# State split that carries the softmax scale, work moved from VectorE to ScalarE and GpSimd, and a new list of steps

## The chip, the cores and the metric

The kernel runs on one core of a Trainium2 chip. The metric is the device time of one execution in microseconds (us). The names of the engines are those of the profile: PE is TensorE's matmul side and PEld its weight load, DVE is VectorE, ACT is ScalarE, POOL is GpSimd, SP is the engine that issues most transfers.

## The reference

Eight batches of eight heads: tokens x (512 x 64 a head) read from a small state (32 x 64 a head), the state reads from the tokens, and the 4608 rows that come out (8 x 512 of the tokens, 8 x 32 of the states, the heads side by side in 512 columns) go through two feed-forward blocks.

```python
def attn(x, state):                      # x [8, 8, 512, 64], state [8, 8, 32, 64]
    scale = 1.0 / np.sqrt(64)
    scores = scale * np.matmul(x, state.transpose(0, 1, 3, 2))
    scores = scores - scores.max(-1, keepdims=True)
    a = np.exp(scores)
    a /= a.sum(-1, keepdims=True) + 1e-09
    xread = np.matmul(a, state)
    scores2 = scale * np.matmul(state, x.transpose(0, 1, 3, 2))
    a2 = softmax(scores2)                # written out as above
    sread = np.matmul(a2, x)
    return np.concatenate([xread, sread], axis=2)

def moe(x, w_in, w_out, g_ln):           # x [4608, 512], w_in [512, 1024], w_out [1024, 512]
    h = x @ w_in
    e = np.exp(h - h.max(-1))
    solu = h * e / (e.sum(-1) + 1e-09)
    ln = (solu - mean(solu)) / np.sqrt(var(solu) + 1e-06) * g_ln
    return ln @ w_out

def moe2(x, w_in, w_out):                # w_in [512, 2048], w_out [2048, 512]
    h = x @ w_in
    return np.maximum(0.01 * h, h) @ w_out
```

## The kernel before

**Precision and shapes.** Most products are computed from pairs of a high and a low part: `hi` is the value as the narrower type fp32r, `lo` is what is left of it, and `mm3` (line 136) issues three passes, hi by hi, hi by lo and lo by hi. A value is split by a copy into `hi` on ACT and a subtraction into `lo` on DVE or POOL. The scores of batches 0 and 1 (`PLAIN_S`) are plain fp32 products without a low part, and their rows of `st` and `sw` show two passes to a product.

**Stages.** Behind the scaled and transposed tokens (`at_xT`, line 335: `xT_hi`, `xT_lo`) and the state as a block matrix (`at_state`, line 293: `stp` in fp32, `stq` in two parts) come the scores of the state (`at_scores`, line 356: `st`, from them `a2`, transposed by PE as `a2t` in `at_a2T`) and the softmax of the tokens (`at_soft1`, line 392: the maximum `mx`, the subtraction into `ee`, the exponential, the sum `sm`, its reciprocal, the product). `at_sw1` and `at_sw2` form the state times the first weights, `w_in` (`sw`), so that `h1` (line 542) has the first product of the block straight from the softmax `a1T`. `solu_norm` (line 502) turns a strip of 128 rows of `h` into the normalised `e`; its statistics sit in little tensors `sn(b, r)` of one or two columns. `turn`, `carry` (line 620) and `x2` (line 648) transpose the strip, split it into `hi` and `lo` in place in `ln`, and multiply by `w_out`. Weights come in raw and are narrowed and split by `narrow_w_in`, `split_w_in` (line 244), `narrow_w_out` and `split_w_out` (line 281). This first phase ends near 400 us; the second block, on sums and differences of quarters of the tokens, fills the rest of the span.

**What sets the order.** Each of these functions is a generator that stops at every `yield`. The string `PROGRAM` (line 1418) is a list of tokens; a letter names the function, the numbers its arguments, and each occurrence carries the generator to its next `yield`: `T` is `at_xT`, `Z` `at_state`, `S` `at_scores`, `U` `at_soft1`, `A` and `B` `at_a2T` and `at_a1T`, `Y` and `W` `at_sw1` and `at_sw2`, `h` `h1`, `V`, `C` and `X` `turn`, `carry` and `x2`, `i` and `j` narrow and split `w_in`, `o` and `p` narrow and split `w_out`. The loop that reads it is at line 1382. Each engine gets its instructions in the order in which the list issues them (`PINNED`) and works through them strictly in that order; nothing is chosen at run time. Transfers are issued by SP's queue in the list's order too.

**At the start** POOL makes the identity matrix for PE's transpositions, clears the two z buffers of the state, all of `stq` (128 x 2048 columns) and `stp`, and PE's first work is the transposition of the state of batch 0.

Of the kernel before, what the change touches and what calls it, by code (L numbers as in the profile page):

```python
# [16 lines left out]
ALU = mybir.AluOpType  # L17
# [12 lines left out]

PLAIN_S = (0, 1)
CARRIED = (1, 2, 3, 4, 5, 6, 7)
LO_ROW_DVE = ()
# [5 lines left out]
def f32(ap):  # L39
    return ap.bitcast(F32)  # L40
# [26 lines left out]
def attn_solu_leaky_kernel(  # L67
# [88 lines left out]
    make_identity(tc.nc, ident)  # L156
    nhalf = slot("nhalf", [P, 1], F32, "nhalf")
    nc.gpsimd.memset(nhalf, -0.5)
# [8 lines left out]
    nc.gpsimd.memset(f32(stq), 0.0)  # L167
# [76 lines left out]
    def split_w_in(k):  # L244
# [5 lines left out]
        nc.gpsimd.tensor_tensor(t[:, 1], w, f32(t[:, 0]), ALU.subtract)  # L250
# [30 lines left out]
    def split_w_out(k):  # L281
# [4 lines left out]
        nc.gpsimd.tensor_tensor(lo, w, f32(hi), ALU.subtract)  # L286
# [6 lines left out]
    def at_state(b, g):  # L293
        for _ in (0,):
# [5 lines left out]
            for m in range(2):  # L300
# [5 lines left out]
                if b in PLAIN_S:  # L306
                    nc.scalar.copy(stp[:, 2 * g + m, d], pt[:, c])
                else:
                    yield from split(stq[:, 0, 2 * g + m, d], stq[:, 1, 2 * g + m, d], pt[:, c])
# [25 lines left out]
    def at_xT(b, hp):  # L335
        if hp == 0:
            att["xT_hi"] = slot("q2", [P, NHP, S], F32 if b in PLAIN_S else F32R, f"xT_hi{b}")
        if b not in PLAIN_S:
# [4 lines left out]
            nc.scalar.activation(hi, t, AF.Copy, scale=SCALE)  # L343
            yield
            nc.vector.scalar_tensor_tensor(lo, t, SCALE, f32(hi), ALU.mult, ALU.subtract)
# [10 lines left out]
    def at_scores(b, g):  # L356
# [26 lines left out]
        nc.vector.tensor_scalar_mul(a2[:, g, :], a2[:, g, :], r2)  # L383
# [8 lines left out]
    def at_soft1(b, g):  # L392
# [8 lines left out]
        nc.vector.tensor_tensor(e3, v, mx.unsqueeze(2).to_broadcast([P, 16, NS]), ALU.subtract)  # L401
# [5 lines left out]
        nc.vector.tensor_scalar_add(sm, sm, EPS_SM)  # L407
# [94 lines left out]
    def solu_norm(key, hp_):  # L502
# [31 lines left out]
        nc.vector.tensor_scalar_mul(c2, cf, rs)  # L534
# [85 lines left out]
    def carry(b, h):  # L620
# [21 lines left out]
        for u in range(2):  # L642
            yield
            hi, lo = (t[:, 4 * h + 2 * u : 4 * h + 2 * u + 2] for t in ln_t[b])
            w = nc.vector if (b, h, u) in LO_ROW_DVE else nc.gpsimd
            w.tensor_tensor(lo, f32(lo), f32(hi), ALU.subtract)
# [772 lines left out]
    a0 i0 i0 i0 z0. i0 i0 Z0.1 Z0.0 Z0.0 a1 i1 x0.0 T0.0 i1 a3 a2 T0.1 T0.0 g Z0.0 i1 i1 i1 z1.  # L1419
    T0.1 S0.0 i3 i2 Y0.0.0 i3 i3 Z0.1 S0.0 S0.0 S0.0 Y0.0.0 Y0.0.1 Y0.0.1 Z0.1 i3 i2 i3 i2 i2 i2  # L1420
    Z1.1 Z1.1 Z1.1 x0.1 T0.2 Z1.0 Z1.0 T0.3 T0.2 T0.3 S0.1 U0.0 j3 Y0.1.0 S0.1 S0.1 Z1.0 U0.1 b0
    o0 Y1.0.0 z2. Z2.0 S0.0 S0.1 S0.1 b2 Y0.1.0 U0.0 o0 S0.0 U0.0 S0.1 Y1.0.0 Z2.0 Y1.0.1 A0.0
    A0.0 A0.1 A0.1 R0 U0.1 Z2.1 o0 U0.0 U0.1 o0 j3 o2 b1 o1 U0.1 o2 R0 Y1.0.1 R0 U0.0 Y0.1.1
    B0.0 R0 Z2.1 Z2.1 Z2.0 o1 Y1.1.1 U0.1 Y1.1.1 B0.1 o0 o1 o2 o1 j2 h0.1 Y0.1.1 h0.1 x1 o2 Z2.1
# [163 lines left out]
```

## Time and profile before

| | us | share of the span |
|---|---|---|
| median of 3 runs (1131.33, 1136.59, 1137.94) | 1136.59 | |
| profiled execution, device time | 1131.78 | |
| its span | 1130.0 | 100% |
| PE busy | 1095.8 | 97% |
| PEld busy (overlaps PE) | 909.5 | 80% |
| DVE busy | 892.2 | 79% |
| POOL busy | 609.2 | 54% |
| ACT busy | 569.0 | 50% |

The profiled execution is 4.8 us under the median of the three. Busy time counts instructions and is an average over stages that differ: DVE is at 9 and 8 tenths in the first eighth of the span and at 5 to 8 behind it. A row of a timeline says when a group of instructions began and how long it took, a row of the list of lines how long one takes on average, and a row of the waits how long an engine stood still and which result it stood for.

### The profile page before, as it was taken

Reading aid. Unit: us, or ns where it says so; the run is one execution under the profiler, and the core shown is the slowest. Engines: PE = TensorE matmul, PEld = TensorE weight load, DVE = VectorE, ACT = ScalarE, POOL = GpSimd, SP = SyncE. Lnnn points to the kernel's source line nnn. Section 1 sums busy time; section 2 is a strip of 40 time slices with the busy share of each in tenths; the row PEclk is TensorE's granted clock in tenths of the full one; section 3 lists DMA queues with packets and bytes.
Section 4 is the critical chain, followed back from the end, with each engine's and each line's share of the span. In section 5 each row is a group of like instructions: output and inputs, shape, how many; then the busy total and the mean of one; then the engine's idle time right before and its main releaser. Section 6 shows DMA issues by size and latency. Waiting matters only on the chain.

```text
span 1130.0 us, 16127 instructions
## 1 busy us (share of the span) xinstructions
PE 1095.8 (97%) x5872; PEld 909.5 (80%) x5872; DVE 892.2 (79%) x1374; ACT 569.0 (50%) x907; POOL 609.2 (54%) x439
## 2 busy tenths in 40 slices
PE   6999999999999999999999989999999999999997
PEld 2555587888788778888888879998889998899987
DVE  7999988887985585667776977888967778776777
ACT  5687687676677374544234343334443335433331
POOL 2234353262462645576647268878665655745463
PEclk9999999999999999999999999999999999999999
DMA  9447989789589856646449577666794658646352
GB/s 303 126 116 195 212 220 214 202 183 266 162 206 269 241 189 227 219 146 228 159 153 333 219 273 277 244 258 236 280 357 192 261 205 316 231 187 253 131 196 75
DMA packets 170647, 247.48 MB, mean 219 GB/s; under 512 B 93128, under 2 KB 129992, under 8 KB 159560
## 3 DMA queue, kind: packets, MB, share of 16 engines
q1 hardware_dynamic: 170568, 246.45, 67.3%
q8 instruction: 46, 0.75, 0.3%
q14 instruction: 33, 0.27, 0.1%
HBM read 171.97 MB, written 74.45 MB: 218 GB/s over the span
## 4 chain that ended last, share of the span: by engine, by line
PE 57%; DMA 2%; issue 1%; POOL 1%; DVE 1%; ACT 0%; POOLq 0%; DVEq 0%; SPq 0%; ACTq 0%
PE hX L53 15%; PE oX L53 11%; PE o L53 10%; PE hY L53 7%; PE oY L53 5%; PE hZ L53 4%; PE oZ L53 2%; PE h L53 2%; PE x L53 1%; DMA xbT<-xts 1%; DMA wf<-wf2s 1%; DMA xbB<-xs 1%; POOL gb L53 0%; DVE C L53 0%; POOL xbT L53 0%
## 5 line engine op out<-in xcount | busy, mean ns | idle before, releaser
L53 DVE TENSOR_TENSOR oacc<-oacc,oX 128x512 f32<-128x512 f32 x171 | 116.0, 683 | 51.2 <-PE oX L53 50.4
L53 PE MATMUL x<-ln,w_out_hi 128*128 128x512 f32 (+1 forms) x512 | 152.7, 382 | 1.4 <-DVE sw L53 1.4
L53 PE MATMUL hX<-xbT,w 128*128 128x512 f32 x576 | 150.2, 396 | 1.8 <-ACT C L53 1.4
L53 ACT COPY C<-hX 128x512 f32<-128x512 f32 x96 | 56.2, 586 | 145.8 <-PE hX L53 142.6
L53 PEld LDWEIGHTS hX<-xbT,w 128*128 128x128 f32 x576 | 103.1, 188 | 21.9 <-ACT C L53 2.4
L53 PEld LDWEIGHTS x<-ln,w_out_hi 128*128 128x128 f32 x512 | 93.4, 188 | 20.7 <-DVE sw L53 1.6
L53 PE MATMUL h<-sw,a1T 128*128 128x512 f32 x352 | 102.8, 437 | 2.5 <-DVE sw L53 1.3
L53 PE MATMUL x<-ln,w_out_lo 128*128 128x512 f32 (+1 forms) x256 | 97.0, 379 | 0.0
L53 POOL TENSOR_TENSOR gb<-C,gb 128x512 fp32r<-128x512 f32 (+1 forms) x43 | 69.2, 1613 | 44.9 <-ACT gb L53 22.5
L53 POOL TENSOR_TENSOR gc<-C,gc 128x512 fp32r<-128x512 f32 (+1 forms) x43 | 67.7, 1577 | 43.8 <-ACT gc L53 20.1
L53 PEld LDWEIGHTS h<-sw,a1T 128*128 128x128 f32 x352 | 64.7, 188 | 30.5 <-issue 14.3
L53 DVE TENSOR_TENSOR C<-C,hY 128x512 f32<-128x512 f32 x64 | 43.9, 686 | 48.8 <-ACT C L53 42.3
L53 DVE SCALAR_TENSOR_TENSOR C<-C 128x512 f32<-128x512 f32 x88 | 78.7, 896 | 0.4
L53 POOL TENSOR_TENSOR ln<-ln,ln 128x1024 fp32r<-128x1024 f32 x28 | 69.1, 2480 | 17.9 <-ACT ln L53 17.8
L53 DVE TENSOR_TENSOR oacc<-oacc,o 128x512 f32<-128x512 f32 x70 | 46.1, 682 | 25.5 <-PE o L53 25.2
L53 DVE TENSOR_TENSOR oacc<-oacc,oY 128x512 f32<-128x512 f32 x93 | 63.1, 681 | 2.4 <-PE oY L53 1.6
L53 PEld LDWEIGHTS x<-ln,w_out_lo 128*128 128x128 f32 x256 | 48.2, 188 | 9.7
L53 POOL TENSOR_TENSOR gb<-S,gb 128x512 fp32r<-128x512 f32 x27 | 43.1, 1604 | 18.2 <-ACT gb L53 11.0
L53 POOL TENSOR_TENSOR gc<-S,gc 128x512 fp32r<-128x512 f32 x26 | 38.9, 1507 | 25.7 <-ACT gc L53 18.8
L53 PE MATMUL hY<-xbT,w 128*128 128x512 f32 x192 | 49.7, 394 | 0.2 <-DVE C L53 0.2
L53 PE MATMUL hX<-xbB,w 128*128 128x512 f32 x192 | 49.6, 393 | 0.0
L53 PE MATMUL hY<-xbB,w 128*128 128x512 f32 x192 | 49.5, 393 | 0.0
(672 smaller groups left out, 2774.4 us busy)
## 6 DMA issues: line engine op xcount, KB each, us to landing
w<-w2s SPq DMA_DIRECT2D x24, 1792.0 KB, 10.1
shared<-wo2s SPq DMA_DIRECT2D x24, 768.0 KB, 4.4
wi<-wsc SPq DMA_DIRECT2D x14, 1024.0 KB, 6.1
exd<-v SPq DMA_DIRECT2D x14, 1024.0 KB, 6.0
ln<-exd SPq DMA_DIRECT2D x56, 256.0 KB, 6.0
xs<-xo SPq DMA_DIRECT2D x34, 256.0 KB, 4.0
raw<-in_moe_w_in SPq DMA_DIRECT2D x8, 1024.0 KB, 6.2
raw<-in_moe_w_out SPq DMA_DIRECT2D x8, 1024.0 KB, 6.4
```

The source lines that it names most:

```text
L53: done = call(*args, **kw)
```

## The change

Six things change together.

1. **Scale.** For batches 2 to 7 the factor 1/8 leaves `at_xT`: `xT_hi` becomes a plain copy of the transposed tokens and `xT_lo` a plain subtraction. It goes into the two parts of the state (`stq`: a scaled copy on ACT, and one fused scale and subtract on DVE in place of a subtract), and, since the tokens' softmax is then multiplied by a state that is scaled, into the divisor of that softmax (`sm`, one fused add and multiply in place of an add).
2. **Off DVE.** For batches with two-part scores the subtraction into `xT_lo` and the subtraction of the maximum in `at_soft1` go to POOL; for batches 1 to 7 the two-column product `c2` in `solu_norm` goes to POOL; for all batches the division of `a2` goes to ACT.
3. **Pieces.** The POOL subtractions of 1024 columns in `split_w_in`, `split_w_out` and `carry` become two of 512 columns each, every piece a step of its own in the list.
4. **Warm-up.** 24 products of zeros with zeros run on PE before anything else, on 512 columns of `stq` that POOL clears first; the identity and the rest of `stq` follow.
5. **New list.** The steps of the first phase, up to about 400 us, stand in a new order; the list behind it is the old one.
6. Per engine the totals go from 1340 to 1260 instructions on DVE, 823 to 839 on ACT, 439 to 541 on POOL and 5656 to 5680 on PE.

```diff
+WARM = 24
-    make_identity(tc.nc, ident)
-    nc.gpsimd.memset(nhalf, -0.5)
 ...
-    nc.gpsimd.memset(f32(stq), 0.0)
+    nc.gpsimd.memset(f32(stq[:, 0, :2, :]), 0.0)
+    warm = bank("warm")
+    zeros = stq[:, 0, :2, :].rearrange("p a b -> p (a b)")
+    for _ in range(WARM):
+        nc.tensor.matmul(warm, zeros[:, :P], zeros, start=True, stop=True)
+    drop("warm")
+    make_identity(tc.nc, ident)
+    nc.gpsimd.memset(nhalf, -0.5)
+    nc.gpsimd.memset(f32(stq[:, 0, 2:, :]), 0.0)
+    nc.gpsimd.memset(f32(stq[:, 1]), 0.0)
 ...                                             # split_w_in; split_w_out alike
-        nc.gpsimd.tensor_tensor(t[:, 1], w, f32(t[:, 0]), ALU.subtract)
+        for i in range(2):
+            if i:
+                yield
+            c = slice(i * 512, (i + 1) * 512)
+            nc.gpsimd.tensor_tensor(t[:, 1, c], w[:, c], f32(t[:, 0, c]), ALU.subtract)
 ...                                             # at_state, batches 2 to 7
-                    yield from split(stq[:, 0, 2 * g + m, d], stq[:, 1, 2 * g + m, d], pt[:, c])
+                    hi, lo = (stq[:, j, 2 * g + m, d] for j in range(2))
+                    nc.scalar.activation(hi, pt[:, c], AF.Copy, scale=SCALE)
+                    yield
+                    nc.vector.scalar_tensor_tensor(lo, pt[:, c], SCALE, f32(hi), ALU.mult, ALU.subtract)
 ...                                             # at_xT, batches 2 to 7
-            nc.scalar.activation(hi, t, AF.Copy, scale=SCALE)
-            yield
-            nc.vector.scalar_tensor_tensor(lo, t, SCALE, f32(hi), ALU.mult, ALU.subtract)
+            nc.scalar.copy(hi, t)
+            yield
+            nc.gpsimd.tensor_tensor(lo, t, f32(hi), ALU.subtract)
 ...                                             # at_scores
-        nc.vector.tensor_scalar_mul(a2[:, g, :], a2[:, g, :], r2)
+        nc.scalar.activation(a2[:, g, :], a2[:, g, :], AF.Copy, scale=r2)
 ...                                             # at_soft1
-        nc.vector.tensor_tensor(e3, v, mx.unsqueeze(2).to_broadcast([P, 16, NS]), ALU.subtract)
+        w = nc.vector if b in PLAIN_S else nc.gpsimd
+        w.tensor_tensor(e3, v, mx.unsqueeze(2).to_broadcast([P, 16, NS]), ALU.subtract)
 ...
-        nc.vector.tensor_scalar_add(sm, sm, EPS_SM)
+        if b in PLAIN_S:
+            nc.vector.tensor_scalar_add(sm, sm, EPS_SM)
+        else:
+            nc.vector.tensor_scalar(sm, sm, EPS_SM, SCALE, ALU.add, ALU.mult)
 ...                                             # solu_norm
-        nc.vector.tensor_scalar_mul(c2, cf, rs)
+        if key[0] in CARRIED:
+            nc.gpsimd.tensor_tensor(c2, cf, rs.to_broadcast([P, 2]), ALU.mult)
+        else:
+            nc.vector.tensor_scalar_mul(c2, cf, rs)
 ...                                             # carry
-        for u in range(2):
-            yield
-            hi, lo = (t[:, 4 * h + 2 * u : 4 * h + 2 * u + 2] for t in ln_t[b])
-            w = nc.vector if (b, h, u) in LO_ROW_DVE else nc.gpsimd
-            w.tensor_tensor(lo, f32(lo), f32(hi), ALU.subtract)
+        for u in range(4):
+            yield
+            hi, lo = (t[:, 4 * h + u] for t in ln_t[b])
+            nc.gpsimd.tensor_tensor(lo, f32(lo), f32(hi), ALU.subtract)
 ...                                             # PROGRAM, its first line
-    a0 i0 i0 i0 z0. i0 i0 Z0.1 Z0.0 Z0.0 a1 i1 x0.0 T0.0 i1 a3 a2 T0.1 T0.0 g Z0.0 i1 i1 i1 z1.
+    a0 i0 i0 i0 i0 a1 i1 x0.0 z0. T0.0 T0.1 a3 i0 T0.0 a2 Z0.0 i1 Z0.0 Z0.0 Z0.1 Z0.1 i1 T0.1
```

What the new list and the moved operations do to the engines' queues is seen at three places. The first is PE behind the first scores, of the kernel before: `sw_g_n` is the state times half g of the rows and half n of the columns of `w_in` (batch 0, and later batch 1 under the same name), `sw_141` the narrowed first half of `w_in` that such a product reads and `sw_192` the second half; `zt` is the transposed state, `xt` the transposed tokens, `st` the scores of the state, `a2t` the transposed softmax of them.

```order
L53 MATMUL sw_0_0_197<-sw_141,stp 128x512 x2
L53 MATMUL sw_0_1_208<-sw_141,stp 128x512 x2
L53 MATMUL zt_1_219<-ident,z_84 128x128
L53 MATMUL xt_2_227<-ident,xn 128x128 x4
L53 MATMUL zt_0_232<-ident,z_84 128x128
L53 MATMUL xt_3_235<-ident,xn 128x128 x4
L53 MATMUL st_1_242<-xT_hi_164,stp 128x512 x2
L53 MATMUL sw_1_0_250<-sw_192,stp 128x512 x2
L53 MATMUL sw_0_0_265<-sw_141,stp 128x512 x2
L53 MATMUL zt_0_272<-ident,z_83 128x128
L53 MATMUL sw_0_1_288<-sw_141,stp 128x512 x2
L53 MATMUL a2t_0_291<-ident,q_93 128x128 x4
```

The same place of the change; here `sw_168` is the first half of `w_in` and `sw_216` the second.

```order
L53 MATMUL sw_0_0_219<-sw_168,stp 128x512 x2
L53 MATMUL sw_0_1_222<-sw_168,stp 128x512 x2
L53 MATMUL xt_3_230<-ident,xn 128x128 x4
L53 MATMUL xt_2_241<-ident,xn 128x128 x4
L53 MATMUL zt_0_258<-ident,z_79 128x128
L53 MATMUL st_1_272<-xT_hi_185,stp 128x512 x2
L53 MATMUL zt_1_280<-ident,z_79 128x128
L53 MATMUL sw_0_1_290<-sw_168,stp 128x512 x2
L53 MATMUL sw_1_1_310<-sw_216,stp 128x512 x2
L53 MATMUL sw_1_0_322<-sw_216,stp 128x512 x2
L53 MATMUL a2t_1_334<-ident,q_120 128x128 x4
L53 MATMUL a2t_0_339<-ident,q_120 128x128 x4
```

Before, the first product that reads the second half of `w_in` (`sw_1_0_250`) came right behind the second scores; now a product of batch 1 that reads the first half (`sw_0_1_290`) comes between, both products of batch 0 that read the second half stand together, and `a2t` follows them at once. (Ahead of these rows stand the 24 warm-up products, and the tokens are transposed before the state.)

The second place is POOL in the stretch in which the halves of the softmax of batch 1 (`ee`) meet the last pieces of `w_out_lo` and the statistics `sn` of batch 1, of the kernel before:

```order
L53 TENSOR_TENSOR ee_739<-ee_739,sm_0_794 128x512
L53 TENSOR_TENSOR w_out_lo<-w_out_f,w_out_hi 128x1024
L53 TENSOR_TENSOR ee_739<-ee_739,sm_1_822 128x512
L53 TENSOR_TENSOR a1T_840<-q_93,a1T_840 128x512
L53 TENSOR_TENSOR w_out_lo<-w_out_f,w_out_hi 128x1024
L53 TENSOR_TENSOR a1T_840<-q_93,a1T_840 128x512
L53 TENSOR_SCALAR sn(1, 3)_800<-sn(1, 3)_800 128x1
L53 TENSOR_TENSOR sn(1, 3)_800<-sn(1, 3)_800,nhalf 128x1
L53 TENSOR_SCALAR sn(1, 1)_816<-sn(1, 1)_816 128x1
L53 TENSOR_TENSOR sn(1, 1)_816<-sn(1, 1)_816,nhalf 128x1
L53 TENSOR_TENSOR w_out_lo<-w_out_f,w_out_hi 128x1024 x2
```

and of the change, where batch 2's tokens are already being split (`xT_lo`, four subtractions):

```order
L53 TENSOR_TENSOR xT_lo<-q_120,xT_hi_627 128x512 x4
L53 TENSOR_TENSOR w_out_lo<-w_out_f,w_out_hi 128x512
L53 TENSOR_TENSOR ee_772<-q_120,mx_1_773 128x512
L53 TENSOR_TENSOR w_out_lo<-w_out_f,w_out_hi 128x512
L53 TENSOR_SCALAR sn(1, 2)_701<-sn(1, 2)_701 128x1
L53 TENSOR_TENSOR sn(1, 2)_701<-sn(1, 2)_701,nhalf 128x1
L53 TENSOR_TENSOR ee_772<-q_120,mx_0_803 128x512
L53 TENSOR_TENSOR sn(1, 2)_701<-sn(1, 2)_701 128x2
L53 TENSOR_SCALAR sn(1, 0)_649<-sn(1, 0)_649 128x1
L53 TENSOR_TENSOR sn(1, 0)_649<-sn(1, 0)_649,nhalf 128x1
L53 TENSOR_TENSOR ee_772<-ee_772,sm_1_848 128x512
L53 TENSOR_TENSOR sn(1, 0)_649<-sn(1, 0)_649 128x2
```

The pieces of `w_out_lo` are half as large and stand between operations that the scores and the softmax of batch 2 need, and each strip's chain of `sn` ends on POOL with the two-column product that DVE had.

The third place is DVE in the same stretch, before:

```order
L53 TENSOR_TENSOR sw_780<-sv_3_1_918,sw_780 64x512
L53 SCALAR_TENSOR_TENSOR xT_lo<-q_93,xT_hi_930 128x512
L53 STREAM_TRANSPOSE q_93<-xv_499 128x512
L53 TENSOR_TENSOR sw_758<-sv_2_1_938,sw_758 64x512
L53 TENSOR_TENSOR sw_758<-sv_3_1_918,sw_758 64x512
L53 TENSOR_TENSOR sw_780<-sv_2_0_933,sw_780 64x512
L53 SCALAR_TENSOR_TENSOR xT_lo<-q_93,xT_hi_930 128x512
L53 TENSOR_SCALAR sn(1, 3)_800<-sn(1, 3)_800 128x2
L53 TENSOR_TENSOR sw_780<-sv_2_1_938,sw_780 64x512
L53 TENSOR_SCALAR sn(1, 1)_816<-sn(1, 1)_816 128x2
```

and in the change:

```order
L53 STREAM_TRANSPOSE q_120<-xv 128x512
L53 TENSOR_TENSOR sw_784<-sv_3_0_906,sw_784 64x512
L53 COPY srT<-sr_941 64x4x32
L53 TENSOR_TENSOR sw_732<-sv_3_1_913,sw_732 64x512
L53 STREAM_TRANSPOSE v_928<-e(1, 2)_719 128x32x32
L53 TENSOR_TENSOR sw_732<-sv_3_0_906,sw_732 64x512
L53 STREAM_TRANSPOSE v_928<-e(1, 1)_935 128x32x32
L53 TENSOR_TENSOR sw_732<-sv_2_0_980,sw_732 64x512
L53 TENSOR_TENSOR sw_732<-sv_2_1_984,sw_732 64x512
L53 STREAM_TRANSPOSE v_928<-e(1, 3)_875 128x32x32
L53 STREAM_TRANSPOSE q_120<-xv_493 128x512
L53 TENSOR_TENSOR sw_784<-sv_2_1_984,sw_784 64x512
```

The rows `xT_lo` and the two-column `sn` rows are gone from DVE's queue, and the transpositions `q` of the tokens and the sums `sw` stand directly behind one another.

## Rows read from the trace of the kernel before

**Rows 1.** Windows: from:to, length, busy us (count) of five engines, PEclk, DMA, GB/s.
```profile
0.00:25.00 25.00, 14.68 (x40) 6.91 (x41) 17.59 (x21) 12.21 (x23) 6.13 (x12) 1.00 0.97 299
25.00:125.00 100.00, 94.24 (x371) 54.81 (x369) 97.41 (x185) 75.47 (x135) 33.29 (x31) 1.00 0.61 156
125.00:350.00 225.00, 219.78 (x1007) 174.72 (x1008) 194.62 (x371) 162.92 (x267) 91.58 (x83) 1.00 0.85 211
350.00:1130.00 780.00, 767.09 (x4458) 673.08 (x4456) 582.58 (x799) 318.42 (x484) 478.23 (x314) 1.00 0.63 227
```

**Rows 2.** Waits of PE, 25 to 425 us: us in total, times, longest.
```profile
PE st L53 <- DVE xT_lo L53: 1.7, 2, 1.1
PE tr L53 <- DVE stq L53: 1.5, 1, 1.5
PE sv L53 <- DVE sw L53: 1.5, 1, 1.5
...
PE h L53 <- DVE sw L53: 1.3, 2, 0.8
```

**Rows 3.** Timelines of DVE, POOL, PE, 117 to 126: start, length, [idle <- releaser].
```profile
117.64 0.68 DVE L53 SCALAR_TENSOR_TENSOR xT_lo<-q,xT_hi 128x512 fp32r<-128x512 f32 x1
118.24 2.34 DVE L53 TENSOR_SCALAR sn(1, 3)_800<-sn(1, 3)_800 128x2 f32<-128x2 f32 x1
...
121.11 0.21 DVE L53 TENSOR_SCALAR sn(1, 1)_816<-sn(1, 1)_816 128x2 f32<-128x2 f32 x1
...
117.65 2.91 POOL L53 TENSOR_TENSOR w_out_lo<-w_out_f,w_out_hi 128x1024 fp32r<-128x1024 f32 x1
...
122.79 0.40 PE L53 MATMUL st<-xT_lo,stq 128*128 128x512 f32 x1
123.03 1.03 PE L53 MATMUL st<-xT_hi,stq 128*128 128x512 f32 x2
125.21 0.51 PE L53 MATMUL st<-xT_lo,stq 128*128 128x512 f32 x1 [1.15 <-DVE xT_lo L53]
```

**Rows 4.** Lines by form, DVE, 0 to 425: busy us, mean ns | idle before.
```profile
L53 DVE SCALAR_TENSOR_TENSOR xT_lo<-q,xT_hi 128x512 fp32r<-128x512 f32 x24 | 16.7, 699 | 0.8 <-ACT xT_hi L53 0.8
...
L53 DVE TENSOR_TENSOR ee<-q,mx 128x512 f32<-128x512 f32 x16 | 10.8, 679 | 0.0
...
L53 DVE TENSOR_SCALAR q<-q,sa 128x512 f32<-128x512 f32 x16 | 7.9, 500 | 0.2
...
L53 DVE TENSOR_TENSOR stq<-zt,stq 128x64 fp32r<-128x64 f32 x24 | 4.5, 209 | 0.2
...
L53 DVE TENSOR_SCALAR sn(6, 1)_2749<-sn(6, 1)_2749 128x2 f32<-128x2 f32 x1 | 2.4, 2357 | 0.2 <-POOL sn(6, 1)_2749 L53 0.2
```

**Rows 5.** Lines by form, POOL and then ACT, 0 to 425 us.
```profile
L53 POOL TENSOR_TENSOR ln<-ln,ln 128x1024 fp32r<-128x1024 f32 x28 | 69.1, 2480 | 17.9 <-ACT ln L53 17.8
L53 POOL TENSOR_TENSOR ee<-ee,sm 128x512 f32<-128x512 f32 x16 | 18.0, 1126 | 42.9 <-DVE sm L53 23.0 <-DVE sn(3, 1)_1450 L53 8.7 <-ACT junk L53 5.6
L53 POOL TENSOR_TENSOR a1T<-q,a1T 128x512 fp32r<-128x512 f32 x12 | 15.7, 1319 | 13.7 <-ACT a1T L53 13.7
...
L53 POOL TENSOR_TENSOR sn(0, 1)_401<-sn(0, 1)_401,nhalf 128x1 f32<-128x1 f32 x1 | 0.6, 556 | 0.1
...
L53 ACT ACTIVATE w_out_f<-w_out_f,gln 128x512 f32<-128x512 f32 x8 | 5.3, 715 | 0.0
```

**Rows 6.** Timelines of the start: PE, then DVE, then POOL.
```profile
12.29 2.95 PE L53 MATMUL st<-xT_hi,stp 128*128 128x512 f32 x4
...
21.28 1.98 PE L53 MATMUL st<-xT_hi,stp 128*128 128x512 f32 x4 [0.36 <-ACT xT_hi L53]
23.57 3.67 PE L53 MATMUL sw<-sw,stp 128*128 128x512 f32 x8 [0.30 <-DVE sw L53]
...
22.20 1.23 DVE L53 SCALAR_TENSOR_TENSOR sw<-raw_in,wi 128x1024 uint32<-128x1024 uint32 x1
...
1.73 1.80 POOL L53 MEMSET stq<- 128x2048 f32 x1
```

## What the change should do to the time

> **What bounds the kernel now.** I read the busy time of each engine by stretches first [rows 1]. Before 350 us TensorE (PE) is idle for 10.3 us (0 to 25), 5.8 us (25 to 125) and 5.2 us (125 to 350), 21.3 us in all, under 2% of the span. That is about the ceiling of this change: behind 350 us the list of steps is nearly the old one, and PE is busy there for 767.1 of 780 us.
>
> The same rows name the engine that paces PE early on: VectorE (DVE) is busy 97.4 of 100 us in 25 to 125 and 194.6 of 225 us after that, against 75.5 and 162.9 us for ScalarE (ACT) and only 33.3 and 91.6 us for GpSimd (POOL). The waits of PE after 25 us agree: four of the rows that stand highest there end on a DVE result and hold 6.0 us in six waits [rows 2]; what each of them waits for either leaves DVE in this change or stands in its queue behind something that leaves.
>
> Then I looked at what DVE did just before such a wait [rows 3]. At 118.24 a two-element multiplication on DVE lasts 2.34 us; one of the same kind at 121.11 takes 0.21 us. It began while a 128x1024 GpSimd subtraction ran (117.65, 2.91 us) and ended with it. Everything behind it on the DVE queue moved back, among it the xT_lo for which PE then stood still until 125.21 (1.15 us). An ordinary DVE operation on two SBUF tensors started at 117.64 under the same subtraction and kept its 0.68 us. So a small DVE scaling can be held for the length of a GpSimd piece, and a plain two-input operation is not. The list by form has another held one, 2.36 us [rows 4].
>
> A wait costs PE a little more than its own length: passes that follow each other start 0.24 us apart and last 0.40 us (122.79, 123.03), so 0.16 us of overlap is lost, and the first pass after the wait lasts 0.51 us (125.21). That is 0.27 us on top of each wait.
>
> **The change, part by part.** Off DVE go 24 xT_lo subtractions (0.699 us each, 16.8), 16 scalings of a2 (0.500, 8.0), 12 of the 16 subtractions of the maximum (0.679, 8.1) [rows 4] and 28 two-element scalings at 0.21 us (5.9) [rows 3], with at least the 4.3 us by which two of them were held. Sum 43 us: DVE falls in 25 to 350 from 292.0 to 249 of 325 us, from 90% to 77%. The 24 scaled splits of the state have no row. The subtraction that each replaces takes 0.209 us; an operation of the new kind on eight times the columns takes 0.699 us [rows 4]. Size and input are the old ones, so I take 0.21 us, no change; the upper end, 24 x 0.49 = 12 us, would still leave DVE at 80%.
>
> Onto ACT go 16 scalings; the nearest row is a scaling by a vector, 0.715 us [rows 5], 11.4 us. ACT rises from 238.4 to 250 of 325 us, 77%: as full as DVE then, not as DVE was.
>
> Onto POOL go 24 xT_lo subtractions at 1.319 us (the a1T row has their shape and types), 31.7; 12 subtractions of a broadcast maximum at 1.126 us (the ee row has their shape, also with a broadcast operand), 13.5; and 28 two-element products, between the 0.21 us of DVE and the 0.556 us of the costliest kind of small GpSimd operation in the rows; I take 0.3, 8.4, with 15.6 as the upper end. 36 subtractions of 1024 columns at 2.480 us become 72 at 1.319, 36 x 0.158 = 5.7 us more [rows 5]. Sum 59 us: POOL rises in 25 to 350 from 124.9 to about 184 us, 57%. What the split buys is that a held DVE operation waits for 1.3 us at most instead of 2.5.
>
> Folding the scale into the state's split and into the divisor costs nothing more: it sits in a ScalarE copy and in a small DVE operation that are there already, and that have other work of PE in front of them. The copy into xT_hi stays on ACT at its size.
>
> At the start 24 warm-up passes run while PE would wait for data. GpSimd clears two z tiles and 512 columns of stq first (a quarter of the 1.80 us row), so they begin near 1.9 us. At 0.24 us a pass they end at 7.7 us, at half that rate at 13.4; the nearest row is one at half rate, so I take a mixture, 10 us, about when x arrives. What they are for shows in two rows [rows 6]: the same four score passes take 2.95 us at 12.29 and 1.98 us at 21.28. A pass of that size takes 0.46 us (3.67 us for eight), so 2.95 is two passes at the lower of the two levels (1.2 GHz) and two at 2.4 GHz, though the clock column of the stretch says 1.00 [rows 1]. Gain at most 1.0 us. The Trainium skill (TensorE: Matmul & The Clock Gate, Part 1) has the clock follow how busy the array has been lately and fall back after idling. By that rule a pause between the warm-up and the arrival of x could give the 1.0 us back; no row here shows such a fall.
>
> The new list also moves one sw product of batch 1 (four passes, 1.8 us) ahead of the first sw that needs the second half of w_in. That half leaves DVE at 23.4 us, and PE stood 0.30 us for it [rows 6]. The DVE work in front of it is the same in both lists, so PE wins what it gets done before 23.5 us. The transposition of a2, soon after in the list, then waits for the new ACT scaling, behind other ACT operations of about 0.7 us. I take 1.0 us for the whole start. Its ends are 2.8 (1.0 + 1.8) and -2.2: passes at half rate until 13.4, then eight transpositions (1.2, the rate of the short passes), a copy (0.7) and the scores (1.98), at 17.3 instead of 15.1.
>
> For 25 to 350: I take away the six waits [rows 2], 6.0 us, and 6 x 0.27 = 1.6 us of restarts. The other waits stay. New is that xT_lo leaves GpSimd 0.62 us later than it left DVE (1.319 - 0.699), in front of the scores of batches 2 to 7. If a third of the six show it, 2 x 0.62 = 1.2 us.
>
> Sum: 1.0 + 6.0 + 1.6 - 1.2 = 7.4 us. The profiled execution took 1131.8 us (span 1130.0 and 1.8 around it) and would become 1124.4; it lies 4.8 us under the median of the runs, 1136.6, so the forecast for the median is 1129.2.
>
> **Rivals.** A measurement of this kernel can tell about 1% (11.4 us) from no change.
>
> *Nearly every stall goes.* With DVE at 77% the remaining waits fall too: 11.0 us of idle in 25 to 350, with a dozen restarts 14, and 1 to 2 us at the start: 15 us, 1121. For it: DVE is the one full queue beside PE. Against it: every engine runs its list strictly in order, so each misjudged duration makes a new stall.
>
> *As dense as the old list.* The stalls of the new order are as many, at other places: 1133 to 1138. For it: POOL now holds more links of each chain.
>
> *GpSimd is late.* The slower side. Batches 2 to 7 have six moved operations each (four xT_lo, two subtractions). Each can find a 1.319 us piece in front of it and itself takes 0.62 or 0.45 us longer than on DVE: 6 x 1.319 + 4 x 0.62 + 2 x 0.45 = 11.3 us a batch, 68 us for six, most of it covered by PE's other work. It decides from where less than about two thirds are covered: a third is 22.6 us, less the 8.6 us won, 14.0 us slower, 1151. For it: POOL's queue is in order, and pieces of w_out_lo now stand between the xT_lo pieces. Against it: POOL at 57%. The Trainium skill (GPSIMD Engine Reference, Engine selection) speaks for this rival: it puts elementwise work on VectorE and calls GpSimd about twice as slow with two inputs. The rows agree on the price (1.319 against 0.699 us), not on the conclusion, because VectorE is the full queue here.
>
> *The warm-up does the opposite*: start -2.2 instead of 1.0, 1132.4; within the forecast's class.
>
> **How the numbers follow.** Forecast, 3 to 11 us faster, with the warm-up's rival: 0.42. Nearly every stall goes: 0.38. As dense as the old: 0.11. GpSimd is late: 0.09. So faster by over 1%: 0.38; within 1%: 0.42 + 0.11 = 0.53; slower by over 1%: 0.09. The likeliest alone spans 1125 to 1134. The 80% range reaches over the second and third; the runs before spread over 6.6 us, half of which goes on top at either end: 1121 less 3, and less 3 more for a start at its high end, is 1115; 1138 and 3 is 1141.
>
> **What would show it.** Right: DVE near 77% busy in 25 to 350, no small DVE operation over about 1.5 us, PE's idle there under 6 us, xT_lo on POOL near 1.3 us, the first sw products at 15 us as before. Wrong: PE waits that end on POOL's xT_lo or ee (GpSimd late) or on ACT's a2 scaling; a first transposition of x after 10.5 us; or PE's idle behind 350 us changed by over 2 us.

## The result, and the profile after

| | before | changed |
|---|---|---|
| first comparison, median (us) | 1135.18 (1131.33 to 1137.94, 4 runs) | 1118.45 (1118.31 to 1120.78, 3 runs) |
| ratio, 95% interval | | 0.9861, 0.9820 to 0.9903 |
| second comparison (the run `again` below), median (us) | 1132.43 (14 runs) | 1121.22 (5 runs) |
| ratio, 95% interval | | 0.9924, 0.9889 to 0.9959 |
| profiled execution, span (us) | 1130.0 | 1119.2 |
| first product of the second block (`hX`), start (us) | 420.83 | 408.37 |

The change is faster by 0.8% to 1.4% by the two ratios, 11 to 17 us by the medians. The forecast was 1129.2 us, 7.4 us faster; the time came out inside the range and at the rival "nearly every stall goes" (1121). The changed kernel's first profiled execution ran at a mean granted clock of 0.65 (1558 us) and is left out of the table; all rows of it below are from the run `again`.

Windows of the changed kernel, answering to [rows 1] (same columns; the last stretch ends with the span):

```profile
0.00:25.00 25.00, 20.59 (x64) 11.99 (x65) 17.22 (x22) 12.20 (x22) 4.50 (x14) 1.00 0.90 290
25.00:125.00 100.00, 97.86 (x389) 58.53 (x388) 91.68 (x172) 81.07 (x145) 50.32 (x54) 1.00 0.67 182
125.00:350.00 225.00, 223.88 (x1049) 181.07 (x1048) 164.84 (x317) 174.82 (x285) 127.47 (x160) 1.00 0.88 214
350.00:1119.00 769.00, 758.51 (x4400) 665.63 (x4399) 579.98 (x784) 309.26 (x472) 476.46 (x316) 1.00 0.62 226
```

PE is idle for 2.1 and 1.1 us in the second and third stretch, 3.3 us where it was 11.0 us. Over these two stretches DVE went from 292.0 to 256.5 of 325 us (79%; the forecast was 77%), ACT from 238.4 to 255.9, POOL from 124.9 to 177.8. (The first stretch's PE time holds the 7.9 us of warm-up.)

Waits of PE in the changed kernel, 25 to 425 us, the whole list (waits from 0.2 us up); it answers to [rows 2]:

```profile
PE tr L53 <- DVE e(0, 2)_617 L53: 0.9, 1, 0.9
PE xt L53 <- DVE srT L53: 0.7, 1, 0.7
PE zt L53 <- DMA z<-in_state: 0.5, 1, 0.5
PE sv L53 <- DMA wi<-wsc: 0.5, 1, 0.5
PE a2t L53 <- ACT q L53: 0.5, 1, 0.5
PE tr L53 <- DVE e(8, 0)_3375 L53: 0.3, 1, 0.3
PE x L53 <- DMA xv<-in_x: 0.2, 1, 0.2
```

None of the rows of [rows 2] is left, and none of PE's waits ends on POOL. One of the signs that the prediction had named as wrong is there, a wait on ACT's scaling of a2 (`a2t <- ACT q`), with 0.5 us. The lines by form of the changed kernel, 0 to 425 us, price what was moved, beside [rows 4, 5]; the groups are POOL's, DVE's and ACT's:

```profile
L53 POOL TENSOR_TENSOR ln<-ln,ln 128x512 fp32r<-128x512 f32 x56 | 73.4, 1342 | 10.2 <-ACT ln L53 7.1 <-DMA xs<-xo 1.5 <-DMA z<-in_state 1.3
L53 POOL TENSOR_TENSOR xT_lo<-q,xT_hi 128x512 fp32r<-128x512 f32 x24 | 31.4, 1315 | 18.6 <-ACT xT_hi L53 18.2
...
L53 POOL TENSOR_TENSOR ee<-q,mx 128x512 f32<-128x512 f32 x12 | 13.4, 1119 | 13.4 <-DVE mx L53 7.1 <-DVE sn(6, 0)_2605 L53 3.6 <-PE h L53 2.7
...
L53 POOL TENSOR_TENSOR sn(1, 3)_858<-sn(1, 3)_858 128x2 f32<-128x2 f32 x1 | 0.2, 199 | 0.1
...
L53 DVE SCALAR_TENSOR_TENSOR stq<-zt,stq 128x64 fp32r<-128x64 f32 x24 | 5.0, 210 | 2.0 <-ACT stq L53 1.9
...
L53 ACT ACTIVATE q<-q,sa 128x512 f32<-128x512 f32 x16 | 11.4, 720 | 0.0
```

Every price of the forecast holds: xT_lo 1.315 us (forecast 1.319), the subtraction of the maximum 1.119 (1.126), a2 on ACT 0.720 (0.715), the scaled split of the state 0.210 (0.21), a piece 1.342 (1.319), and the two-column product 0.20 us on POOL (0.3). What these moves did to PE is another matter, and the experiments are about that.

### The profile page after: what moved, and what is told of

Same layout as the page of the kernel before. It is cut to its first block, busy times and chain, and to the rows that moved or that the text cites. A ratio compares the mean times of both kernels' runs of the same rounds, so it can differ in the third digit from the quotient of the medians.

```text
span 1556.3 us, 16263 instructions
## 1 busy us (share of the span) xinstructions
PE 1548.8 (100%) x5896; PEld 1117.3 (72%) x5896; DVE 853.1 (55%) x1294; ACT 580.5 (37%) x923; POOL 642.7 (41%) x541
## 4 chain that ended last, share of the span: by engine, by line
PE 99%; ACT 0%; POOL 0%; DVE 0%; DVEq 0%; issue 0%; ACTq 0%; POOLq 0%
PE x L53 18%; PE hX L53 16%; PE oX L53 12%; PE h L53 11%; PE o L53 10%; PE hY L53 8%; PE oY L53 6%; PE hZ L53 4%; PE oZ L53 3%; PE sr L53 3%; PE st L53 2%; PE sv L53 2%; PE sw L53 1%; PE hs L53 1%; PE a2t L53 1%; PE warm L53 1%
## 5 line engine op out<-in xcount | busy, mean ns | idle before, releaser
L53 PE MATMUL hX<-xbT,w 128*128 128x512 f32 x576 | 205.2, 506 | 0.0
L53 PE MATMUL x<-ln,w_out_hi 128*128 128x512 f32 (+1 forms) x512 | 204.7, 493 | 0.0
L53 PE MATMUL h<-sw,a1T 128*128 128x512 f32 x352 | 147.3, 582 | 0.0
L53 PE MATMUL x<-ln,w_out_lo 128*128 128x512 f32 (+1 forms) x256 | 125.5, 490 | 0.0
L53 POOL TENSOR_TENSOR ln<-ln,ln 128x512 fp32r<-128x512 f32 x56 | 72.7, 1328 | 34.7 <-ACT ln L53 34.7
L53 PE MATMUL hY<-xbB,w 128*128 128x512 f32 x192 | 68.7, 510 | 0.0
L53 PE MATMUL hX<-xbB,w 128*128 128x512 f32 x192 | 68.6, 506 | 0.0
L53 PE MATMUL hZ<-xbB,w 128*128 128x512 f32 x192 | 68.6, 506 | 0.0
L53 PE MATMUL hY<-xbT,w 128*128 128x512 f32 x192 | 68.5, 510 | 0.0
L53 PE MATMUL o<-misc,gc 128*128 128x512 f32 x192 | 66.5, 508 | 0.0
```

Source lines behind the costliest of these rows:

```text
L53: done = call(*args, **kw)
```

## The experiments

Two theories stood against each other at first. **Theory P** is the prediction's: the placement does it, since DVE's queue was full and small scalings on it were held. **Theory L**: the new list does it. A third was that the start carries the unforeseen part. `old_list` and `old_work` undo one half of the change each, `c2_1024` and `nowarm1024` two parts together; the others are the changed kernel with one part undone or moved. The milestone is the start of the first `hX`: it ends the first phase, and what follows it takes 709 us in the kernel before and 711 in the changed one. Ratios are to the kernel before, timed beside each run.

**again**, the changed kernel without an edit.

> The changed kernel once more, for an undisturbed profile beside the kernel before. Measured in the first comparison: 1118.3 to 1120.8 us where the kernel before had 1131.3 to 1137.9. Every theory expects about 1119 us and a ratio of 0.986 again. The theory of the prediction (DVE was full, small scalings on it were held by long GpSimd pieces, both are gone) expects DVE near 77% busy in 25 to 350 us, and, as the gain is twice the forecast, PE's idle there under 3 us of the 11.0 us of before. A theory that the gain lies elsewhere (the start, or behind 350 us) expects PE's idle in 25 to 350 us still above 6 us and a start or a tail shorter by 5 us or more.

1121.22 us, ratio 0.9924 (0.9889 to 0.9959); its rows are above. PE's idle from 25 to 350 us is 3.3 us, a little over the 3 that was expected and far under the 6 of the other theory, so the gain is where the prediction looked for it.

**old_list**: the new code with the old list.

```diff
 PROGRAM = """
-    a0 i0 i0 i0 i0 a1 i1 x0.0 z0. T0.0 T0.1 a3 i0 T0.0 a2 Z0.0 i1 Z0.0 Z0.0 Z0.1 Z0.1 i1 T0.1
+    a0 i0 i0 i0 z0. i0 i0 Z0.1 Z0.0 Z0.0 a1 i1 x0.0 T0.0 i1 a3 a2 T0.1 T0.0 g Z0.0 i1 i1 i1 z1.
...
```

> The changed kernel with the old list of steps; the two 512-column pieces of a split then follow each other in one step. Theory P (placement: off DVE, short pieces): most of the gain stays, 1122 to 1126 us, since the queue of DVE is as relieved as with the new list. Theory L (list: the new order is what fits the durations): the old order was made for the old placement and is now wrong for POOL's longer operations, 1132 us or more, no faster than before.

1133.27 us, ratio 1.0013 (0.9989 to 1.0036), milestone 423.56 us: no gain at all. Waits of PE in `old_list`, 25 to 425 us, and its windows from 25 to 350:

```profile
PE h L53 <- POOL a1T L53: 2.1, 1, 2.1
...
PE hs L53 <- DVE srs L53: 1.7, 1, 1.7
PE h L53 <- DVE sn(5, 0)_2170 L53: 1.5, 1, 1.5
PE sr L53 <- ACT ee L53: 1.4, 2, 1.2
PE a2t L53 <- ACT q L53: 1.1, 1, 1.1
```

```profile
25.00:125.00 100.00, 95.15 (x375) 55.88 (x374) 89.83 (x170) 79.60 (x142) 42.24 (x49) 1.00 0.60 156
125.00:350.00 225.00, 221.00 (x996) 174.99 (x995) 159.28 (x309) 165.92 (x271) 128.86 (x154) 0.98 0.84 210
```

DVE is as relieved as the prediction had it (89.8 + 159.3 = 249.1 us of 325, 77%; forecast 249), and most of the old waits are gone from the list. New ones stand in their place, on POOL's a1T, on ACT's scaling of a2 and on the ends of chains, and one of 2.0 us for DVE's `sw` at 24.58 us (left out above). In all PE is idle for 10.9 us from 25 to 425 us, where it was 12.6; against that, the granted clock was 0.66 from 280 to 290 us, which costs 3.4 us. Theory P as it stood falls.

**old_work**: the new list and the warm-up, all work back in its old place (xT_lo with its scale as shown, and alike `stq`, `sm`, `ee`, `a2`, `c2` and the pieces of 1024 columns).

```diff
-            nc.scalar.copy(hi, t)
+            nc.scalar.activation(hi, t, AF.Copy, scale=SCALE)
             yield
-            nc.gpsimd.tensor_tensor(lo, t, f32(hi), ALU.subtract)
+            nc.vector.scalar_tensor_tensor(lo, t, SCALE, f32(hi), ALU.mult, ALU.subtract)
...
```

> The changed kernel with the new list and the warm-up, but every moved operation back in its old place: scale in xT_hi and xT_lo, xT_lo, the subtraction of the maximum, the division of a2 and c2 on DVE, GpSimd subtractions of 1024 columns. Theory P: the gain is gone, 1134 to 1145 us, DVE above 88% busy in 25 to 350 us, and small DVE scalings held for about 2 us again. Theory L: most of the gain stays, 1120 to 1126 us.

1166.62 us, ratio 1.0304 (1.0272 to 1.0336), milestone 457.55 us. Theory L falls too, and harder: the new list with the old placement loses 34 us on the kernel before, more than theory P had allowed. Waits of PE in `old_work`, the whole span, the first rows:

```profile
PE a2t L53 <- DVE q L53: 8.3, 4, 2.4
PE x L53 <- DVE stq L53: 3.8, 1, 3.8
PE sr L53 <- DVE sw L53: 3.0, 1, 3.0
PE st L53 <- DVE xT_lo L53: 2.6, 2, 1.7
```

PE is idle for 35.3 us from 25 to 425 us, 22.7 more than before, and falls of the granted clock (0.66 from 120 to 130 us, for one) cost 11.9 us more. DVE, with its old work, is busy for 85% of 25 to 350 us, not the 88% that was expected: it waits too. Four of its two-column products are held for 1.9 to 2.4 us, as expected. Neither half brings anything alone; the list fits the new placement and not the old one. What is left to ask is which moves the list needs.

**no_warm**: the 24 products left out.

```diff
...
-    for _ in range(WARM):
-        nc.tensor.matmul(warm, zeros[:, :P], zeros, start=True, stop=True)
...
```

> The changed kernel without the 24 warm-up products; GpSimd's order at the start stays. The prediction's size of the warm-up is 1.0 us at most: 1120 to 1121 us, and the first scores of the state take 2.95 us instead of 1.98. The rival that the start carries the unforeseen part of the gain: 1124 us or more. The rival that the warm-up delays the start: 1117 to 1118 us.

1120.27 us, ratio 0.9896 (0.9868 to 0.9923): the same time. Timelines of PE at the start, first of the changed kernel, then of `no_warm` (columns as in [rows 3]):

```profile
1.79 7.90 PE L53 MATMUL warm<-stq 128*128 128x512 f32 x24 [1.79 <-POOL stq L53]
...
12.17 1.98 PE L53 MATMUL st<-xT_hi,stp 128*128 128x512 f32 x4 [0.25 <-ACT stp L53]
13.99 3.69 PE L53 MATMUL sw<-sw,stp 128*128 128x512 f32 x8
...
21.14 0.33 PE L53 MATMUL zt<-ident,z 128*128 128x128 f32 x1 [0.69 <-ACT xT_hi L53]
...
28.70 0.27 PE L53 MATMUL a2t<-ident,q 128*128 128x128 f32 x1
```

```profile
12.58 3.36 PE L53 MATMUL st<-xT_hi,stp 128*128 128x512 f32 x4
15.77 3.60 PE L53 MATMUL sw<-sw,stp 128*128 128x512 f32 x8
...
21.15 0.33 PE L53 MATMUL zt<-ident,z 128*128 128x128 f32 x1 [0.69 <-ACT xT_hi L53]
...
28.71 0.27 PE L53 MATMUL a2t<-ident,q 128*128 128x128 f32 x1
```

The warm-up does what it is for: the scores take 1.98 us instead of 3.36, and the first `sw` begins 1.8 us earlier. At 21.14 and 21.15 us both stand at the same place, having waited 0.69 us for the same result made from the second half of the tokens. The lead is spent there.

The next four kernels undo single moves. **Theory H**: small DVE scalings are held by long GpSimd pieces. **Theory Q**: only the amount of work in DVE's queue counts.

**c2_dve**: the 28 two-column products back on DVE.

```diff
-        if key[0] in CARRIED:
-            nc.gpsimd.tensor_tensor(c2, cf, rs.to_broadcast([P, 2]), ALU.mult)
-        else:
-            nc.vector.tensor_scalar_mul(c2, cf, rs)
+        nc.vector.tensor_scalar_mul(c2, cf, rs)
```

> The changed kernel with one thing undone: the 28 two-column products c2 back on DVE (0.21 us each where nothing holds them, 5.9 us in all, under 2% of DVE's time in the first phase). Theory H (holding): a small DVE scaling waits until the GpSimd piece that runs beside it ends, here 1.3 us at most; several of the 28 last 0.8 us or more, and the time is 1122 to 1126 us. Theory Q (only the amount of work in DVE's queue counts): 1120 to 1122 us, as the changed kernel's 1121.

1141.95 us, ratio 1.0106 (1.0052 to 1.0159), milestone 431.72 us: 21 us by the medians for 5.9 us of work, far over both theories, though six of the 28 last 1.05 to 1.25 us as theory H has it. The trace tells where the time went. Timelines of `c2_dve` near 107 us: POOL, DVE, then PE.

```profile
106.93 0.19 POOL L53 TENSOR_SCALAR sn(1, 3)_858<-sn(1, 3)_858 128x1 f32<-128x1 f32 x1 [4.95 <-ACT junk L53]
107.20 0.55 POOL L53 TENSOR_TENSOR sn(1, 3)_858<-sn(1, 3)_858,nhalf 128x1 f32<-128x1 f32 x1
...
103.53 0.21 DVE L53 TENSOR_SCALAR sn(1, 3)_858<-sn(1, 3)_858 128x1 f32<-128x1 f32 x1
107.78 0.23 DVE L53 TENSOR_SCALAR sn(1, 3)_858<-sn(1, 3)_858 128x2 f32<-128x2 f32 x1 [4.05 <-POOL sn(1, 3)_858 L53]
107.92 1.30 DVE L53 STREAM_TRANSPOSE q<-ee 128x512 f32<-128x512 f32 x2
109.25 0.69 DVE L53 TENSOR_TENSOR sw<-sv,sw 64x512 fp32r<-64x512 f32 x1
...
110.00 6.53 PE L53 MATMUL sr<-ee,xn 128*128 128x64 f32 x32 [3.00 <-DVE sw L53]
```

The product takes 0.23 us and is not held. But it reads a result that ACT (the sum of squares) and POOL (the power) still have to make, so DVE stands still for 4.05 us at the head of its queue, and the transpositions and the `sw` behind it stand with it, though what they read was ready earlier (POOL's last `ee` ended at 101.97 us, ACT's copy into `sw` at 104.66). PE then waits 3.00 us. The summed rows of DVE's waits that end on POOL's `sn`, 25 to 425 us, are 19.7 us in nine waits here, the longest 4.9, and 0.7 us in one in the changed kernel.

The wait is not all. Windows of `c2_dve` around the stretches in which the clock column fell:

```profile
20.00:30.00 10.00, 9.16 (x22) 3.99 (x21) 7.99 (x13) 7.01 (x15) 2.50 (x2) 0.83 0.76 238
110.00:120.00 10.00, 10.00 (x37) 7.93 (x38) 6.34 (x12) 5.67 (x10) 3.73 (x5) 0.53 0.30 58
120.00:130.00 10.00, 10.00 (x33) 5.98 (x32) 9.74 (x12) 5.11 (x9) 7.64 (x7) 0.96 0.93 237
180.00:190.00 10.00, 8.11 (x29) 6.39 (x29) 6.95 (x14) 9.88 (x16) 2.71 (x3) 0.83 1.04 278
240.00:260.00 20.00, 18.04 (x88) 14.85 (x87) 11.45 (x25) 13.87 (x24) 14.24 (x13) 0.91 0.87 150
340.00:360.00 20.00, 18.12 (x76) 14.31 (x75) 11.23 (x23) 12.57 (x21) 7.27 (x10) 0.91 0.89 239
```

Behind the 3.00 us wait PE is fully busy (10.00 of 10 us) and gets through 37 passes at a granted clock of 0.53, nearly all of the stretch at the lower of the two levels (1.2 GHz). Length times the missing share of the clock gives 1.7, 4.7, 0.4, 1.7, 1.8 and 1.8 us, 12.1 us in all. With 9 us more of idle PE (25 to 425 us: 12.3 against 3.5) that is 21 of the 23.3 us by which the milestone is later. The 1.7 us at 20 to 30 us, though, lie ahead of the first of the moved products (98.75 us), and `piece1024` has them too; some 10 of the 12.1 us go with c2.

**piece1024** and **c2_1024**: GpSimd pieces of 1024 columns (`split_w_out` shown, the other two alike), without and with c2 on DVE.

```diff
-        for i in range(2):
-            if i:
-                yield
-            nc.gpsimd.tensor_tensor(lo[:, i], w[:, i], f32(hi[:, i]), ALU.subtract)
+        nc.gpsimd.tensor_tensor(lo, w, f32(hi), ALU.subtract)
+        yield
...
```

> The changed kernel with one thing undone: the GpSimd subtractions of w_in, w_out and ln in 1024 columns, at the place of the first half in the list. Theory H: few small scalings are left on DVE, but those that are (the divisor of the softmax, the statistics) can be held for 2.5 us instead of 1.3, and xT_lo on POOL finds a piece twice as long ahead of it: 1122 to 1127 us. Theory Q: DVE's amount of work is the same and POOL has 5.7 us less: 1119 to 1121 us.

> Both of the other two undone at once: c2 on DVE and GpSimd pieces of 1024 columns. Theory H: the 28 small scalings meet pieces of 2.5 us; several last over 2 us as in the kernel before, and the cost is more than the sum of the two costs alone: 1127 to 1135 us. Theory Q: 1120 to 1122 us.

`piece1024`: 1119.65 us, ratio 0.9912 (0.9881 to 0.9942), the changed kernel's time. `c2_1024`: 1142.90 us, ratio 1.0101 (1.0048 to 1.0154), the time of `c2_dve` and outside what either theory expected. Holding is real: the 34 two-column products of the first phase take DVE 13.2 us in `c2_dve` with none over 1.25 us, and 16.7 us in `c2_1024` with three of 2.3 to 2.4 us. It does not reach the end of the kernel. As the cause of c2's cost theory H falls.

**xtlo_dve**: the 24 subtractions into xT_lo back on DVE.

```diff
-            nc.gpsimd.tensor_tensor(lo, t, f32(hi), ALU.subtract)
+            nc.vector.tensor_tensor(lo, t, f32(hi), ALU.subtract)
```

> The changed kernel with one thing undone: the 24 subtractions into xT_lo back on DVE (16.8 us at 0.699 us), the scale still in the state. Theory Q: DVE's queue is 16.8 us longer between 60 and 310 us, PE's waits on DVE come back there: 1126 to 1135 us. The rival of the prediction that a slower xT_lo on POOL costs time (GpSimd late): 1117 to 1120 us, faster than the changed kernel. Theory H alone (two-input subtractions are not held): 1120 to 1123 us.

1130.84 us, ratio 1.0000 (0.9975 to 1.0025), milestone 419.19 us: the whole gain is gone, inside the range that theory Q gave. Waits of PE in `xtlo_dve`, 25 to 425 us:

```profile
PE h L53 <- DVE sw L53: 2.2, 2, 1.5
PE st L53 <- DVE xT_lo L53: 1.9, 2, 1.5
```

Two of the rows of [rows 2] are back. DVE is busy for 266 us in 25 to 350 us (92.1 + 174.0; 256.5 in the changed kernel), and the clock column stays at 1.00 there. So the new list needs xT_lo on POOL. That the amount of work on DVE is the reason is not shown. Four of the 24 subtractions last 0.91 to 1.53 us, the others 0.65 to 0.69; the four are those that began while a POOL piece ran, so these subtractions, with two inputs, are held too, against what theory H had assumed, and the wait of 1.5 us for `sw` comes behind the longest of them (on DVE at 116.60 us). `mx_dve` and `a2_dve` below put half as much work back each, for 1 and 4 us by the medians.

The last four ask whether a wait at the head of DVE's queue (**theory W**) explains c2, how large the other two moves are, and whether two idle parts covered for each other.

**c2_late**: c2 on DVE, issued one step later (the edit as against `c2_dve`; batches 0 and 8 stay where they were).

```diff
-        nc.vector.tensor_scalar_mul(c2, cf, rs)
+        if key[0] not in CARRIED:
+            nc.vector.tensor_scalar_mul(c2, cf, rs)
         yield
         if key[0] in CARRIED:
+            nc.vector.tensor_scalar_mul(c2, cf, rs)
             nc.scalar.activation(e, e, AF.Identity, bias=c2[:, 1:2], scale=c2[:, 0:1])
```

> As c2_dve (1142 us: the 28 two-column products on DVE), but each is issued one step of the list later, directly ahead of the ScalarE operation that reads it, so that more of DVE's other work stands in front of it. Theory W (head of the queue: DVE stands still at the product until ScalarE and GpSimd have finished the strip's statistics, and all behind it waits): DVE's waits for sn on POOL shrink from 4.05 us at the longest to under 1.5 us, and at least half of the 21 us comes back: 1121 to 1131 us. Theory H (holding by GpSimd pieces) and theory Q (amount of work) see the same operations on the same engine: 1138 to 1144 us.

1147.89 us, ratio 1.0148 (1.0106 to 1.0191), milestone 442.60 us. The expectation was missed, and the time lies outside the ranges of all three theories: DVE's waits for POOL's `sn` do shrink (7.0 us in three, the longest 2.9 where under 1.5 was expected), and nothing comes back. Waits of ACT in `c2_late`, 25 to 425 us:

```profile
ACT e(2, 1)_1046 L53 <- DVE sn(2, 1)_1039 L53: 4.2, 2, 2.1
ACT e(4, 3)_1957 L53 <- DVE sn(4, 3)_1954 L53: 4.1, 1, 4.1
ACT e(6, 3)_2641 L53 <- DVE sn(6, 3)_2606 L53: 4.1, 1, 4.1
```

The wait has moved one queue on. The waits of ACT's operations on `e` for `sn`, batches 1 to 7, sum to 9.2 us in the changed kernel, 22.5 in `c2_dve` and 41.3 here; with DVE's it is 10, 42 and 48 us. The chain runs ACT, POOL, DVE, ACT: with the product on DVE it needs DVE's turn as well, and whichever of the two queues comes first stands still for the other. On POOL the product follows the power at once. That the wait as such costs the time is in line with this but not shown by itself; whether a list made for c2 on DVE would do without the wait was not tried.

**mx_dve** and **a2_dve**: the subtraction of the maximum, and the division of a2, back on DVE.

```diff
-        w = nc.vector if b in PLAIN_S else nc.gpsimd
+        w = nc.vector
```

```diff
-        nc.scalar.activation(a2[:, g, :], a2[:, g, :], AF.Copy, scale=r2)
+        nc.vector.tensor_scalar_mul(a2[:, g, :], a2[:, g, :], r2)
```

> The changed kernel with one thing undone: the 12 subtractions of the maximum back on DVE (0.679 us each, 8.1 us). They follow DVE's own reduction, so nothing of another engine is waited for. Theory Q, by the 10 us that 16.8 us of xT_lo cost: 4 to 6 us more than the changed kernel, 1124 to 1128 us. Theory W: no wait at the head of DVE's queue is added, 1119 to 1122 us.

> The changed kernel with one thing undone: the 16 divisions of a2 back on DVE (0.500 us each, 8.0 us, against some 11 us on ScalarE). Theory Q: 4 to 6 us more than the changed kernel, 1124 to 1128 us. Theory W: they follow DVE's own reciprocal, nothing is added at the head of the queue, 1119 to 1122 us.

`mx_dve`: 1122.07 us, ratio 0.9918 (0.9886 to 0.9950), by the ratio not to be told from the changed kernel; `a2_dve`: 1125.43 us, ratio 0.9949 (0.9922 to 0.9976). By medians the first lies at the edge of theory W's range, the second in theory Q's. Their milestones are at 415.43 and 416.19 us, 7 and 8 us later than the changed kernel's in one profile each, 1.7 and 3.4 us of it in falls of the clock, of which `a2_dve` has one ahead of all it changes (20 to 30 us). At the end of those profiles it is 2.6 and 3.7 us, since the changed kernel's has a longer wait for `gc` behind the milestone (2.4 us, here 0.8 and 1.1) and a fall of the clock behind that wait (1.7 us). The medians say 1 and 4 us, from two comparisons. So each of the two moves brings little, and how little is open.

**nowarm1024**: no warm-up and 1024-column pieces together.

> The changed kernel without the warm-up and with GpSimd pieces of 1024 columns: the two parts that cost and brought nothing alone, undone together. If they are truly idle parts: 1118 to 1121 us, as the changed kernel. If one covered for the other: 1123 us or more.

1124.21 us, ratio 0.9933 (0.9907 to 0.9958). The median lies where "one covered for the other" was expected, 3 us over the changed kernel's in another comparison, but the interval holds the changed kernel's 0.9924, so a cost of some 3 us is neither shown nor excluded. No version was found that beats the changed kernel clear of the noise.

## Why the prediction was right or wrong

**The place was right, the size was not.** PE's idle before 350 us is what the change had to give, and it gave it: the milestone moved by 12.4 us, and behind it the two kernels take 709 and 711 us. The term that was mis-sized is the main one, "I take away the six waits": 6.0 us of the 11.0 us of idle and 1.6 us of restarts went into the sum, and "the other waits stay". They did not: 7.7 of the 11.0 us went. From 25 us to the milestone it is 9.1 us of idle (12.6 to 3.5), and PE's busy time over the same work fell by 3.4 us (383.2 to 379.9), where the restarts would be; that all of it is restarts is not shown. This was the second case (0.38), taken as slightly less likely than the forecast (0.42). The term against it cost nothing: no wait of PE ends on POOL's xT_lo, so the 1.2 us for it were not needed. The sign "PE's idle behind 350 us changed by over 2 us" did appear, 12.9 to 10.5 us, but it tells little: that stretch holds the last 58 to 71 us of the first phase, and behind the milestone it is 11.3 and 10.4 us.

**Part of the gain by the medians was in no term.** The forecast took 7.4 us off the profiled execution and carried its 4.8 us to the median over unchanged. Profile to profile the gain is 10.8 us (1131.78 to 1121.00); the medians say 11 to 17. The kernel before was timed 43 times beside the experiments, and time and mean granted clock go together: 20 of these at a clock of 0.995 or less took 1130.6 to 1141.8 us, 19 at 0.998 or more 1125.4 to 1130.8. The changed kernel stayed at 0.996 to 0.998. At the same 0.998 the two took 1128.8 to 1130.8 us (five) and 1118.3 to 1122.0 us (six), 9 us apart. The rest goes with the clock, which the kernel before loses in many executions and kept in its profiled one (0.999). `old_list` loses it too (0.993 to 0.999, 1128.5 to 1137.8 us).

**The reason was half right.** The prediction said that DVE was the full queue and that relief of it removes the waits. `old_list` has DVE at exactly the forecast 249 us and gains nothing. With the new list `xtlo_dve` loses the gain, so what stands on DVE does count there. What the argument lacked is that the list was treated as a bystander ("every misjudged duration makes a new stall" stood only as an argument against): placement and order bring 1121 us together, 1133 and 1167 us apart. That no new waits took the place of the six is owed to a list that fits the placement; the prediction had no term for that.

**The holding of small scalings was overrated, and the rest of that reading was wrong.** The row of 2.34 us [rows 3] was read rightly, and three more of the two-column products last 1.67 to 2.25 us beside the two that the prediction counted. But the pieces of 512 columns, said to buy shorter holds, buy no time (`piece1024`). "A plain two-input operation is not" held rests on one row, in which DVE began 0.01 us ahead of POOL (117.64 and 117.65). The only xT_lo of the kernel before that began while a POOL subtraction was already running (`ln`, since 239.14 us) took 1.24 us, the others 0.64 to 0.69, and `xtlo_dve` has four more. From the timeline of DVE, 240 to 243 us, of the kernel before:

```profile
240.88 1.24 DVE L53 SCALAR_TENSOR_TENSOR xT_lo<-q,xT_hi 128x512 fp32r<-128x512 f32 x1 [0.35 <-ACT xT_hi L53]
```

Of c2 the prediction counted the work (5.9 us) and the holding (4.3 us) and left out the third thing: what DVE waits for before it can begin. Undone alone, c2 costs 21 us, the most of all the parts; how much of that is this wait was not measured by itself.

**The start brought nothing, not 1.0 us.** The first `a2t` begins at 28.70 us in the changed kernel and at 28.91 before, a lead of 0.2 us; then the other seven wait for ACT's scaling and end at 30.42 us, where all eight had ended at 29.95. First the kernel before, then the changed one:

```profile
28.91 1.04 PE L53 MATMUL a2t<-ident,q 128*128 128x128 f32 x8
```

```profile
29.44 0.98 PE L53 MATMUL a2t<-ident,q 128*128 128x128 f32 x7 [0.46 <-ACT q L53]
```

The 1.0 us for the clock was under rather than over (1.4 us between 3.36 and 1.98 us), and the first `sw` began at 13.99 us, not "at 15 us as before"; the step left out is the next wait, for the second half of the tokens, at 21.1 us with or without.

**The slower rival, GpSimd late, did not come.** POOL is 55% busy in 25 to 350 us (forecast 57%), and xT_lo on DVE is 9.6 us worse. The Trainium skill (GPSIMD Engine Reference, Engine selection) prefers VectorE for elementwise work; the measurement decides otherwise here: a subtraction takes 1.315 us on POOL against 0.699 us on DVE, and yet the kernel with the 24 on DVE takes 1130.84 us against 1121.22.

**The chances** put 0.53 on within 1% and 0.38 on faster by more. With 0.8% and 1.4% in the two comparisons it lies on that border. That the time stayed inside 1115 to 1141 us is owed to the width of that range, which took the second case in; the forecast itself was 8 to 11 us too slow.

## What to carry to other kernels

Where each engine works through a fixed list, an operation can cost what stands still behind it while it waits for its input, and not only its own duration: before pricing a small operation, see which engine makes what it reads, and try it on the engine that makes the last of it. A list of steps and a placement are one change: try each without the other before a gain is put down to either. A wait of the matrix engine is to be counted together with the granted clock of the stretch behind it.

## What the runs showed of the hardware that was not expected

A wait of PE of 3.00 us was followed by about 10 us at the lower clock level, 110 to 120 us at 0.53 in `c2_dve`: it cost 5.1 us on top of the 3.00. The Trainium skill (TensorE: Matmul & The Clock Gate, Part 1) has the clock fall back after idling; these rows agree, and they show that a wait which the prediction priced at its length and 0.27 us can cost nearly three times its length.

Not every wait does. The kernel before has one of 2.92 us in its second phase with the clock at 1.00 behind it; in the changed kernel the same four products come behind a wait of 2.36 us and the clock is 0.83 from 660 to 670 us, at a cost of 1.7 us. First before, then changed:

```profile
677.75 0.74 PE L53 MATMUL oX<-shared,gc 128*128 128x256 f32 x4 [2.92 <-POOL gc L53]
```

```profile
664.89 1.00 PE L53 MATMUL oX<-shared,gc 128*128 128x256 f32 x4 [2.36 <-POOL gc L53]
```

In `c2_dve` a wait of 1.80 us (246.87) was followed by a fall, in `old_work` one of 2.47 us (375.60) by none. So the length of a wait alone does not decide, and one profile of a kernel does not show what its other executions lose.

The clock also fell near 21 us, at the small waits for the second half of the tokens, in five of the ten experiments with the warm-up, in one profile each (0.83 over 20 to 30 us in `c2_dve` above), at a cost of 1.7 us, and in none of the three kernels without it. The changed kernel's own profile is among the five without a fall there. What decides between the two is open.
